# Seven of eight result stores moved from SyncE's queue to GpSimd's in a two-branch attention kernel

## The chip, the cores and the metric

The kernel runs on one core of one Trainium2 chip. The metric is device microseconds from the start to the end of one execution; the comparison value is the median of several runs. Engines are TensorE (PE), VectorE (DVE), ScalarE (ACT), GpSimd (POOL) and SyncE (SP). SP computes nothing here: it issues the transfers between HBM and on-chip memory.

## The reference, cut to what matters

Two attention blocks read their own inputs and their results are put side by side.

```python
def _A_ref(x, k_cache, v_cache, wq, wo):          # 32 query heads, 4 key/value heads
    q = (x @ wq).reshape(B, Sq, Hq, Dh).transpose(0, 2, 1, 3)
    k = jnp.repeat(k_cache, rep, axis=1)          # rep = 8
    v = jnp.repeat(v_cache, rep, axis=1)
    p = _softmax(jnp.einsum("bhqd,bhkd->bhqk", q, k) * (Dh ** -0.5))
    o = jnp.einsum("bhqk,bhkd->bhqd", p, v)
    return o.transpose(0, 2, 1, 3).reshape(B, Sq, Hq * Dh) @ wo
# _B_ref is the same with 32 key/value heads and no repeat
return jnp.concatenate([a, b], axis=-1)
```

B = 16 sequences of Sq = 32 queries, D = 1024, Sk = 1024 keys, Dh = 128, all bf16. Block B's two caches hold 134 MB each and are read once; this is what makes up most of the 337.64 MB that the profile counts as read.

## The kernel before

**Steps.** The work runs in 128 steps (step 0 to 127). Each step handles one B quad (two sequences times two heads) and, a little faster, one A quad (one sequence times four heads), so that A is done with step 123. In the text "scores 124" is the B quad of step 124, "124A" the A quad of that step. For a quad, in this order:

- K arrives in `KB_sb` (8 slots, two transfers of 512 KB a step, line 772; one slot each is called K127a and K127b) and is transposed in place by DVE (line 806);
- PE makes scores into `ps_s` (line 847 for B, 827 for A; two buffers, taken in turn);
- DVE takes the negated maximum (line 857), ACT the exponential into `P_sb` with its sum (line 870);
- PE transposes `P_sb` (line 882), ACT or DVE copies it to `PT_sb` (line 531);
- PE multiplies with V (line 912 for B, 904 for A); V is in `VB_sb` (3 slots of two transfers of 512 KB, line 785);
- the result is scaled into `O_sb` (lines 928, 929), transposed (line 934) and copied to `OTA_sb` or `OTB_sb`.

V of quad n may only be fetched when the V product of quad n-3 has been done, since there are three slots. After four steps of B (eight of A) a group of 128 tokens has all heads of a block of heads, and `oproj` multiplies them with `wo` (line 703: 16 matmuls for A, 8 for B) and adds into the fp32 accumulator `acc`. For the last block of heads the addition (line 717, called accF) writes bf16 back over the front of the accumulator, and the result rows of that group (128 x 1024 bf16, 256 KB) are stored (line 720). There are four groups in A and four in B: eight stores.

**Order.** Every operation is put into a list with its reads and writes. `list_schedule` then simulates all engines with a table of durations and fixes the order on each engine by estimated start, including the order of transfers on SP. Each engine runs its list strictly in order; an operation waits for its semaphores at the head of its engine's list, and everything behind it on that engine waits too. For a store this means: SP stands at the store until DVE has done both accF additions, with the next K and V loads queued behind. All loads and stores are issued by SP and go through one hardware queue (q1). The planner gives a transfer a ready time with a margin:

```python
                if uo.dma_key is not None:
                    r += DMA_MARGIN.get(uo.name, DMA_MARGIN_DEFAULT)
```

At the end SP waits for all transfers. GpSimd makes two identity matrices at the start and then has nothing to do.

Of the kernel before, what the change touches and what calls it, by code (L numbers as in the profile page):

```python
# [10 lines left out]
BF = mybir.dt.bfloat16  # L11
# [429 lines left out]
def build(nc, pa, pb, out):  # L441
    P = 128
    Bn, Sq, D = pa["x"].shape
    NTOK = Bn * Sq
    assert Sq == 32 and Bn % 4 == 0
    NG = NTOK // P
# [21 lines left out]
    out_flat = out.rearrange("b s c -> (b s) c")  # L468
# [3 lines left out]
    cols = [0, D]  # L472

    pr = Prog()
    stack = contextlib.ExitStack()
    with stack:
        def sb(name, shape, dt):
            return stack.enter_context(nc.sbuf_tensor(name, shape, dt))
# [15 lines left out]
        acc = sb("acc", [P, 2, NG, D], F32)  # L494
# [14 lines left out]
        def bank(v):  # L509
            return ps_g[:, v.idx, :]  # L510
# [12 lines left out]
        def evac(dst_ap, src_ap, reads, writes, name, eng=None, wtag=None, rtag=None, mul=None):  # L523
            def emit(e):
                dst = dst_ap() if callable(dst_ap) else dst_ap
                src = src_ap() if callable(src_ap) else src_ap
                if mul is not None:
                    if hasattr(e, "activation"):
                        return e.activation(dst, src, ACTF.Copy, scale=mul)
                    return e.tensor_scalar(dst, src, mul, None, ALU.mult)  # L530
                return e.copy(dst, src) if hasattr(e, "activation") else e.tensor_copy(dst, src)  # L531
            eng = eng or "any"
            pr.add(eng, emit, reads=reads, writes=writes, name=name if eng == "any" else name + "@" + eng, wtag=wtag, rtag=rtag)
# [35 lines left out]
        def lazy_flush(prefix):  # L569
            last = -1  # L570
            for i, (k, _, _) in enumerate(lazy):
                if k[:len(prefix)] == prefix:
                    last = i
            for _ in range(last + 1):
                lazy.pop(0)[1]()
# [113 lines left out]
        def oproj(pi, blk, G):  # L689
            gp = (blk * NG + G) % 2  # L690
            nh = HS if pi == 0 else MS
            nblk = NSB if pi == 0 else NMSB
            OT = OTA_sb if pi == 0 else OTB_sb
            wo_ = woA_sb if pi == 0 else woB_sb
            wo_res = "woA" if pi == 0 else "woB"
            lazy_flush(("wo", pi, blk))
            for oh in range(NOH):
                v = Virt("bank", "pj")
                for h0_ in range(0, nh, 2):
                    def e_op(e, oh=oh, h0_=h0_, v=v):  # L700
                        last = None
                        for hh in range(h0_, h0_ + 2):
                            last = e.matmul(bank(v)[:, 0:OUTW], OT[:, gp, hh, :], wo_[:, hh, oh * OUTW:(oh + 1) * OUTW],  # L703
                                            start=(hh == 0), stop=(hh == nh - 1))
                        return last
                    pr.add("pe", e_op, reads=[("OT", pi, gp, h0_), ("OT", pi, gp, h0_ + 1), (wo_res, h0_), (wo_res, h0_ + 1)], writes=[v],
                           name="oprojA" if pi == 0 else "oprojB",
                           dur=0.45 * OUTW / 512, rtag={(wo_res, h0_): blk, (wo_res, h0_ + 1): blk, ("OTv", pi, gp): (blk, G)})
                a_ap = acc[:, pi, G, oh * OUTW:(oh + 1) * OUTW]
                o_ap = acc[:, pi, G, :].bitcast(BF)[:, oh * OUTW:(oh + 1) * OUTW]  # L710
                if blk == 0:
                    evac(a_ap, lambda v=v: bank(v)[:, 0:OUTW], reads=[], writes=[v, ("acc", pi, G, oh)], name="acc0")
                elif blk < nblk - 1:
                    pr.add("dve", lambda e, a_ap=a_ap, v=v: e.tensor_tensor(a_ap, a_ap, bank(v)[:, 0:OUTW], ALU.add),  # L714
                           reads=[], writes=[v, ("acc", pi, G, oh)], name="acc+")
                else:
                    pr.add("dve", lambda e, a_ap=a_ap, o_ap=o_ap, v=v: e.tensor_tensor(o_ap, a_ap, bank(v)[:, 0:OUTW], ALU.add),
                           reads=[], writes=[v] + [("acc", pi, G, x) for x in range(oh + 1)], name="accF")
            if blk == nblk - 1:
                pr.add("sp", lambda e: e.dma_start(out_flat[G * P:(G + 1) * P, cols[pi]:cols[pi] + D], acc[:, pi, G, :].bitcast(BF)[:, 0:D]),  # L720
                       reads=[("acc", pi, G, x) for x in range(NOH)], dma_key=f"out{pi}_{G}", name="out_dma", dur=P * D * 2)

        class Quad:
# [342 lines left out]
        def stepA(qA):  # L1066
            tA = qA.t % (NG * 8)
            if qA.t == min(1, NIT - 1):
                for hh in pro_heads:
                    qprojA_head(0, hh)  # L1070
                wo_loadA(0)
            quadA_all(qA)
            if qA.last_of_group:
                oproj(0, qA.s, qA.G)
                if qA.G == NG - 1 and qA.s + 1 < NSB:
                    wo_loadA(qA.s + 1)

        for t in range(NIT):
            cur_step[0] = t
            pr.step = t  # L1080
            qB = quadsB[t]
            tB = t % (NG * 4)
            quadB_all(qB)
            target = min(NIT, -(-(t + 1) * NIT // NAS))
            while ia[0] < target:
                stepA(quadsA[ia[0]])
                ia[0] += 1
            tn = t + (4 - t % 4)
            if tn < NIT:
                qn = quadsB[tn]  # L1090
                if t % 4 == 0:
                    qprepB_tr(qn.m, qn.G)
                    qprepB_sh(qn.m, qn.G)
            for what in q_plan.get(t, ()):
                what()
            if qB.last_of_group:
                oproj(1, qB.m, qB.G)
                if qB.G == NG - 1 and qB.m + 1 < NMSB:
                    wo_loadB(qB.m + 1)
            lazy_pop(LAZY_PER_STEP)  # L1100
# [3 lines left out]
        if SCHED:  # L1104
            pr = pr.list_schedule()
# [41 lines left out]
```

## Time and profile before

| what | value |
|---|---|
| median of 3 runs | 891.7 us (891.68 to 892.2) |
| the profiled execution, whole | 894.39 us |
| its span, first to last instruction | 892.3 us |
| PE / DVE / ACT / POOL busy | 92% / 83% / 68% / 0% |
| DMA moved in all | 341.65 MB, mean 383 GB/s over the span |
| mean granted TensorE clock | 0.994 |
| stores: first and last issue | 715.94 us, 888.9 us |
| stores: issue on SP, min / median / max | 0.343 / 0.356 / 1.152 us |

The profiled execution lies 2.7 us above the median, of which the part outside the span is 2.1 us. Times given as "at 871.13" are us from the start of the span. A DMA share at or over 1 means that all 16 DMA engines had work through the whole slice. Single issues on SP last from 0.33 us; much longer ones are read here as standing against a full queue.

### The profile page before, as it was taken

Reading aid. Unit: us, or ns where it says so; the run is one execution under the profiler, and the core shown is the slowest. Engines: PE = TensorE matmul, PEld = TensorE weight load, DVE = VectorE, ACT = ScalarE, POOL = GpSimd, SP = SyncE. Lnnn points to the kernel's source line nnn. Section 1 sums busy time; section 2 is a strip of 40 time slices with the busy share of each in tenths; the row PEclk is TensorE's granted clock in tenths of the full one; section 3 lists DMA queues with packets and bytes.
Section 4 is the critical chain, followed back from the end, with each engine's and each line's share of the span. In section 5 each row is a group of like instructions: output and inputs, shape, how many; then the busy total and the mean of one; then the engine's idle time right before and its main releaser. Section 6 shows DMA issues by size and latency. Waiting matters only on the chain.

```text
span 892.3 us, 29320 instructions
## 1 busy us (share of the span) xinstructions
PE 820.2 (92%) x12864; PEld 469.4 (53%) x12864; DVE 739.5 (83%) x1030; ACT 608.6 (68%) x1347; POOL 1.1 (0%) x8
## 2 busy tenths in 40 slices
PE   6999899999999999999999999999899878978976
PEld 3365565556555455555555555555456545544543
DVE  0398888879987888889898888898899889888985
ACT  3387886776768577675777677676767767565763
POOL 0000000000000000000000000000000000000000
PEclk9999999999999999999999999999999999998999
DMA  9999999999999999999999999999999999999994
GB/s 318 397 395 392 391 393 396 392 389 395 395 366 387 396 395 390 380 393 395 395 393 394 391 393 394 372 395 394 394 378 380 393 395 395 396 394 382 394 374 166
DMA packets 145278, 341.65 MB, mean 383 GB/s; under 512 B 12032, under 2 KB 12032, under 8 KB 145152
## 3 DMA queue, kind: packets, MB, share of 16 engines
q1 hardware_dynamic: 145152, 339.79, 100.7%
q8 instruction: 101, 1.65, 0.8%
q14 instruction: 25, 0.20, 0.1%
HBM read 337.64 MB, written 2.10 MB: 381 GB/s over the span
## 4 chain that ended last, share of the span: by engine, by line
PE 53%; DMA 18%; DVE 14%; ACT 9%; SPq 3%; issue 1%; DVEq 0%; ACTq 0%
DMA KB_sb<-in_B_k_cache_dram 14%; PE ps_s L847 12%; PE ps_g L703 9%; PE ps_g L882 9%; ACT P_sb L870 6%; DVE stat L857 6%; DVE KB_sb L806 6%; PE ps_g L912 5%; PE ps_g L615 4%; PE ps_g L904 4%; PE ps_s L827 3%; PE ps_g L634 3%; PE ps_g L798 2%; ACT PT_sb L531 2%; SPq L785 2%; DMA VB_sb<-in_B_v_cache_dram 1%
## 5 line engine op out<-in xcount | busy, mean ns | idle before, releaser
L857 DVE TENSOR_REDUCE stat<-ps_s 128x1 f32<-128x1024 f32 x256 | 305.4, 1208 | 53.3 <-PE ps_s L847 43.9
L806 DVE STREAM_TRANSPOSE KB_sb<-KB_sb 128x1024 f32<-128x1024 f32 x256 | 310.2, 1230 | 35.8 <-DMA KB_sb<-in_B_k_cache_dram 32.7
L870 ACT ACTIVATE P_sb<-ps_s,stat 128x1024 bf16<-128x1024 f32 x256 | 286.1, 1119 | 60.9 <-DVE stat L857 59.2
L882 PE MATMUL ps_g<-id,P_sb 128*128 128x128 f32 x1024 | 172.7, 295 | 9.7 <-ACT OTA_sb L531 3.2
L847 PE MATMUL ps_s<-KB_sb,QR 32*32 32x512 bf16 x4096 | 160.1, 397 | 23.1 <-ACT P_sb L870 17.4
L882 PEld LDWEIGHTS ps_g<-id,P_sb 128*128 128x128 f32 x1024 | 149.1, 207 | 48.1 <-issue 9.2
L531 ACT COPY PT_sb<-ps_g 128x512 f32<-128x512 f32 x238 | 138.2, 593 | 50.9 <-PE ps_g L882 49.8
L928 ACT ACTIVATE O_sb<-ps_g,stat 128x128 bf16<-128x128 f32 x186 | 67.9, 371 | 62.9 <-PE ps_g L912 36.5
L912 PE MATMUL ps_g<-VB_sb,PT_sb 128*32 128x128 bf16 x4096 | 92.0, 224 | 7.0 <-ACT PT_sb L531 3.6
L847 PEld LDWEIGHTS ps_s<-KB_sb,QR 32*32 32x32 bf16 x4096 | 47.1, 89 | 85.0 <-ACT P_sb L870 27.0
L827 PE MATMUL ps_s<-KTA_sb,QT_sb 128*128 128x512 bf16 x256 | 87.0, 383 | 4.2 <-ACT P_sb L870 4.1
L912 PEld LDWEIGHTS ps_g<-VB_sb,PT_sb 128*32 128x32 bf16 x4096 | 60.5, 97 | 55.3 <-issue 36.4
L904 PE MATMUL ps_g<-VA_sb,PT_sb 128*128 128x128 bf16 x1024 | 77.6, 220 | 3.1 <-ACT PT_sb L531 1.2
L904 PEld LDWEIGHTS ps_g<-VA_sb,PT_sb 128*128 128x128 bf16 x1024 | 61.0, 98 | 31.6 <-issue 13.9
L634 PE MATMUL ps_g<-wq_sb,xT_sb 128*128 128x512 bf16 x256 | 72.8, 388 | 3.9 <-DMA wq_sb<-in_B_wq_dram 3.9
L703 PE MATMUL ps_g<-woB_sb,OTB_sb 128*128 128x512 bf16 x256 | 67.6, 380 | 3.4 <-ACT PT_sb L531 1.3
L703 PE MATMUL ps_g<-woA_sb,OTA_sb 128*128 128x512 bf16 x256 | 62.5, 380 | 0.8 <-DVE OTA_sb L531 0.3
L934 PE MATMUL ps_g<-ident,O_sb 128*128 128x128 bf16 x256 | 52.5, 223 | 4.5 <-ACT O_sb L928 3.6
L615 PE MATMUL ps_g<-xT_sb,wq_sb 128*128 128x512 bf16 x192 | 55.5, 380 | 0.4 <-ACT QR L531 0.2
L870 ACT ACTIVATION_READ_ACCUMULATOR P_sb<-ps_s,stat 128x1 f32 x256 | 51.6, 202 | 0.0
L531 ACT COPY OTA_sb<-ps_g 128x64 f32<-128x64 f32 x114 | 24.5, 216 | 37.2 <-PE ps_g L934 36.6
L714 DVE TENSOR_TENSOR acc<-acc,ps_g 128x512 f32<-128x512 f32 x64 | 41.0, 675 | 8.7 <-PE ps_g L703 8.4
(42 smaller groups left out, 511.9 us busy)
## 6 DMA issues: line engine op xcount, KB each, us to landing
VB_sb<-in_B_v_cache_dram SPq DMA_DIRECT2D x256, 512.0 KB, 12.2
KB_sb<-in_B_k_cache_dram SPq DMA_DIRECT2D x256, 512.0 KB, 12.4
KA_sb<-in_A_k_cache_dram SPq DMA_DIRECT2D x64, 256.0 KB, 12.3
VA_sb<-in_A_v_cache_dram SPq DMA_DIRECT2D x64, 256.0 KB, 12.2
wq_sb<-in_B_wq_dram SPq DMA_DIRECT2D x16, 512.0 KB, 10.5
woB_sb<-in_B_wo_dram SPq DMA_DIRECT2D x32, 256.0 KB, 11.3
woA_sb<-in_A_wo_dram SPq DMA_DIRECT2D x32, 256.0 KB, 9.9
wq_sb<-in_A_wq_dram SPq DMA_DIRECT2D x12, 512.0 KB, 11.3
```

The source lines that it names most:

```text
L531: return e.copy(dst, src) if hasattr(e, "activation") else e.tensor_copy(dst, src)
L615: last = e.matmul(bank(v)[:, 0:tn], w_[:, j, hh * Dh:(hh + 1) * Dh], xT_sb[:, 0, j, t0:t0 + tn], start=(j == 0), stop=(j == DJ - 1))
L634: last = e.matmul(bank(v)[:, 0:CW], xT_sb[:, 1, j, G * P:(G + 1) * P], wq_sb[:, j, mh * CW:(mh + 1) * CW], start=(j == 0), stop=(j == DJ - 1))
L703: last = e.matmul(bank(v)[:, 0:OUTW], OT[:, gp, hh, :], wo_[:, hh, oh * OUTW:(oh + 1) * OUTW], start=(hh == 0), stop=(hh == nh - 1))
L806: pr.add("dve", lambda e: e.transpose(KB_sb[:, sl, :].bitcast(F32), KB_sb[:, sl, :].bitcast(F32)), writes=[("KB", sl)], name="KBt_tr", rta ...
L827: pr.add("pe", lambda e, u=u: e.matmul(ps_s[:, vS.idx, u, :], qt[:, q.b, q.hh0:q.hh0 + 4, :].rearrange("p a q -> p (a q)"), KTA_sb[:, sl, ...
L847: last = e.matmul(ps_s[32 * cg:32 * cg + 32, vS.idx, g2, :].rearrange("p (s j) -> p s j", s=16), lhsT, rhs, start=(fp == 0), stop=(fp == 3 ...
L857: pr.add("dve", lambda e: e.tensor_reduce(stat[:, vst.idx, 0:1], ps_s[:, vS.idx, :, :], AXIS.XY, ALU.max, negate=True), writes=vS.res + [v ...
L870: return e.activation(dst, src, ACTF.Exp, bias=stat[:, vst.idx, 0:1], scale=1.0, accum_out=stat[:, vst.idx, 1:2])
L882: last = e.transpose(bank(vb)[:, m * P:(m + 1) * P], p32[:, m:Sk // 2:NPK], id32[:])
L904: last = e.matmul(bank(vb)[:, 0:Dh], ptc_of(vPT, c, 0, P), VA_sb[:, kvs, c, :], start=(c == 0), stop=(c == NCH - 1))
L912: last = e.matmul(bank(vb)[32 * a:32 * a + 32, 0:Dh], ptc_of(vPT, c, 32 * a, 32 * a + 32), VB_sb[:, kvs, a // 2, a % 2, c, :], start=(c == ...
```

## The change

The store is issued by GpSimd except for the last group of B. Nothing else in the source differs; the order of all engines is planned anew from the new list.

```diff
             if blk == nblk - 1:
-                pr.add("sp", lambda e: e.dma_start(out_flat[G * P:(G + 1) * P, cols[pi]:cols[pi] + D], acc[:, pi, G, :].bitcast(BF)[:, 0:D]),
+                pr.add("sp" if pi == 1 and G == NG - 1 else "pool", lambda e: e.dma_start(out_flat[G * P:(G + 1) * P, cols[pi]:cols[pi] + D], acc[:, pi, G, :].bitcast(BF)[:, 0:D]),
                        reads=[("acc", pi, G, x) for x in range(NOH)], dma_key=f"out{pi}_{G}", name="out_dma", dur=P * D * 2)
```

In the built program GpSimd has seven stores behind its identity matrices, each waiting for DVE, and SP has one. SP's loads stand in the old order up to the tail, where V125 (waiting for the V product of quad 122) comes ahead of the two loads of K127 instead of behind them. On PE, DVE and ACT the order differs in two stretches: around the first two stores (steps 100 to 108) and from about step 121 to the end. In the second, these move:

- PE: the V product of quad 122 stands ahead of that of 123 (it stood behind); the 16 matmuls of A's last `oproj` are mixed with the 8 of B's and stand ahead of scores 125 (they stood behind it, in one piece, ahead of the transposes of quad 124).
- DVE: max 122 stands between the transposes of K123a and K123b (it stood behind both); in the tail the order is accF, accF, K126a, accF, accF, K126b, max 125, K127a, K127b, max 126, max 127 (it was accF, accF, K126a, K127a, K127b, accF, accF, K126b, max 125, max 126, max 127).

## The prediction

> **What bounds the kernel now.** I read the queue's own waits first, since the change takes stores out of SP's list. Columns: us in total, times, longest.
>
> ```profile
> SPq L785 <- PE ps_g L912: 68.3, 33, 6.2
> SPq L785 <- PE ps_s L847: 60.3, 30, 7.8
> SPq L720 <- DVE acc L717: 23.4, 6, 11.0
> ```
>
> SP stands 23.4 us at stores waiting for accF. The 11.0 us is the last store of the kernel, which stays on SP; 12.4 us go. That is worth something only where the DMA engines run dry meanwhile, so the windows come next (PE, PEld, DVE, ACT, POOL busy; clock; DMA share; GB/s).
>
> ```profile
> 712.00:812.00 100.00, 81.54 (x1467) 49.70 (x1455) 89.13 (x124) 66.97 (x149) 0.00 (x0) 0.98 1.04 395
> 812.00:824.00 12.00, 11.97 (x146) 5.61 (x139) 8.92 (x12) 5.22 (x13) 0.00 (x0) 0.91 1.01 369
> 824.00:864.00 40.00, 32.37 (x602) 21.35 (x600) 37.39 (x55) 28.89 (x62) 0.00 (x0) 0.97 1.04 397
> 864.00:888.00 24.00, 20.47 (x360) 10.39 (x359) 15.65 (x22) 10.29 (x25) 0.00 (x0) 0.97 0.61 221
> ```
>
> Up to 864 the DMA engines are full at 395 to 397 GB/s but for one dent, and SP's wait is hidden by transfers already queued. From 864 on they are at 221 GB/s: the tail is no longer set by bandwidth. So I read the tail on SP, PE and DVE in the timeline (start, us).
>
> ```profile
> 855.86 3.71 SPq L772 DMA_DIRECT2D KB_sb<-in_B_k_cache_dram  x4
> 866.99 1.92 SPq L785 DMA_DIRECT2D VB_sb<-in_B_v_cache_dram  x4
> 871.13 0.36 SPq L720 DMA_DIRECT2D out_dram<-acc  x1
> 876.41 0.88 SPq L785 DMA_DIRECT2D VB_sb<-in_B_v_cache_dram  x2
> ```
> ```profile
> 861.90 1.03 PE L912 MATMUL ps_g<-VB_sb,PT_sb 128*32 128x128 bf16 x32 [1.35 <-DMA VB_sb<-in_B_v_cache_dram]
> 870.96 3.63 PE L703 MATMUL ps_g<-woA_sb,OTA_sb 128*128 128x512 bf16 x16
> 874.42 0.63 PE L882 MATMUL ps_g<-id,P_sb 128*128 128x128 f32 x4
> 885.01 0.63 PE L912 MATMUL ps_g<-VB_sb,PT_sb 128*32 128x128 bf16 x32 [0.62 <-ACT PT_sb L531]
> ```
> ```profile
> 871.02 3.49 DVE L806 STREAM_TRANSPOSE KB_sb<-KB_sb 128x1024 f32<-128x1024 f32 x3
> 874.43 1.44 DVE L717 TENSOR_TENSOR acc<-acc,ps_g 128x512 bf16<-128x512 f32 x2
> 875.79 1.24 DVE L806 STREAM_TRANSPOSE KB_sb<-KB_sb 128x1024 f32<-128x1024 f32 x1
> 880.63 1.22 DVE L857 TENSOR_REDUCE stat<-ps_s 128x1 f32<-128x1024 f32 x1 [0.84 <-PE ps_s L847]
> ```
>
> The V product of 123 (861.90) waits for its data, with that of 122, whose data is there, behind it; hence V125 and V126 are issued only at 866.99. A's `oproj` then holds PE in one piece for 3.63 us, its accF comes at 874.43, behind that K126b at 875.79, and then the last three scores. The final max is done at 881.85 and the V product of 127 starts at 885.01, for a copy by ACT and not for a DMA. The end is a chain of engine work in a fixed order, and the change reorders it.
>
> **Part by part. GpSimd's issue.** Seven stores leave SP: issues of 0.36 us (one 1.15 us), some 3.3 us, and 12.4 us of waits. Behind each on SP stood the next K and V loads. At 767 and 843 SP stood 2.7 and 3.6 us, and the DMA stayed full: worth nothing. In 812 to 824 SP stood 2.2 and 1.6 us, and the rate fell to 369 GB/s: (397-369)/397 x 12 = 0.85 us of transfer. Between 824 and 849 the chain of waits runs through engines alone, so I count 0 of it and keep 0.8 for the range. On GpSimd a waiting store holds only the next store. GpSimd's last stores become ready at about 872, 17 us before the end, while a store took at most 11.0 us to land; they end nothing.
>
> **What a GpSimd store costs.** The trace has none. Bounds: below, a gain only if its packets were cheaper than those of SP's store, 0.66 us at 395 GB/s (256 KB), at most 7 x 0.66 = 4.6 us, of which I exclude nearly all, since the bytes and rows are the same. Above, the engines could be held twice as long: 5 stores before the tail, 5 x 0.66 = 3.3 us. The nearest row is SP's own store of the same bytes, so I take 0 and keep part of the 3.3 for the range. The Trainium skill, DMA: Bandwidth & Descriptors, "Issuing engines are not separate DMA queues", says that all issuers share the same 16 engines, and that spreading issues saves only the sequencer's time; by that alone the sum would be 0 (the first rival).
>
> **The new order around the first stores** (716 to about 790). The DMA is full there, and SP's issues of 1 to 4 us show a full queue, so a shift of one or two us on PE costs nothing; 0, at worst a dent like the 0.85 us one.
>
> **The tail**, in the built order and with this trace's durations (transpose 1.16, max 1.2, exp with its sum 1.21, accF 0.69, copy 0.6):
> - DVE from 851.16: K123a, max 122 (to 853.5), K123b, max 122A (855.9). Exp 122 ends at 855.1 where it ended at 856.03; scores 123 to 856.3; max 123 to 857.5; exp 123 to 858.7 where it was 859.74.
> - PE: P 123 transposed by 859.3, then the V product of 122, after its copy, at 859.8 to 860.4. Its slot was free at 866.94. V125 is issued at about 860.5 instead of 866.99, K127 behind it by 863, and the queue doesn't run dry.
> - Max 123, K124a, max 123A, K124b end at 861.0; scores 124 at 862.2 (was 867.3).
> - Then on PE, ahead of P 124: P 123A (0.5), V products 123 and 123A (1.1), two small transposes (0.2), 24 `oproj` matmuls (5.5), scores 125 (1.1): 8.4 us, and 1.0 for waits on the copies into `OTA_sb` and `OTB_sb` (PE's load queue shows 0.9 us for such waits in the tail): scores 125 end at 871.6, `oproj` at 870.5. P 124 is done at 872.2 where it was 875.05, V127 issued at about 874.3 (was 876.41).
> - DVE: last accF pair to 871.9, K126b 873.1, max 125 874.3, K127a and b 876.6, max 126 877.8, max 127 879.0 (was 881.85).
> - Exp 127 to 880.25 (was 883.09). From there to the V product of 127 it was 1.92 us: 882.2 instead of 885.01. V127 landed 4.3 to 5.3 us after issue, so by 880: no wait. Behind it nothing changes: 892.3 - 885.01 = 7.3 us, end of span 889.5.
>
> The gain is 2.8 us: profiled execution 891.6, span 889.5. The median lies 2.7 us under the profiled one: 888.9.
>
> Thinnest cover: K127 now stands behind V125 in the queue. In this stretch K loads took 12.3 to 13.8 us to land, hence K127 by about 871.5 before; 1 MB more ahead at 397 GB/s is 2.6 us: 874.1, needed at 874.3 and 875.4. What it is late goes on the end one for one.
>
> **Rivals.**
> 1. *No change.* The hidden waits are hidden, and the tail's gain of 2.8 us goes into waits that my sum leaves out: in-order ACT (O copies behind exp 124) ahead of the mixed `oproj`, PSUM banks that accF gives back, K127 late by a us. For: each of some fifteen hand-overs needs only 0.1 to 0.15 us more. Against: max 125 alone moves from 876.95 to about 873. Gain 0 to 1.7 us; 891.2.
> 2. *Slower: GpSimd's stores hold the DMA engines.* Place: the 16 engines, full until 864; a second queue takes turns with loads, and loads due next (K125 and V123, for which DVE and PE wait at 862.97 and 861.90) land late by what each store costs beyond its 0.66 us. Five stores come before that point. It decides from (2.8 + 1.8)/5 = 0.9 us extra per store on; at 1.2 us extra, 6.0 - 2.8 = 3.2 us slower, 894.9. Against: no row shows such a cost. The Trainium skill, DMA: Bandwidth & Descriptors, "Latency and other measured facts", calls engines 7 and 15 usually slower and guesses at the ports that hold GpSimd's descriptor rings; that bears on this rival, and no run here shows it yet.
> 3. *More.* The 0.85 us dent comes through as well, and the waits I added are shorter: 3.6 to 4.6 us, 887.6.
>
> That the change doesn't do what it says is excluded by the built order: seven stores stand on GpSimd.
>
> **How the numbers follow.** A measurement of this kernel can tell about 0.2%, 1.8 us, from no change. Forecast 0.47 (888.9, itself 887.5 to 889.9), no change 0.30, slower 0.16, more 0.07. Faster 0.54, same 0.30, slower 0.16. The range goes down to 887.0, past most of "more", and up to 893.5, which takes in "no change" and the mild end of rival 2.
>
> **What would show it.** After: L720 on SP once, with one wait; a dent near 816 smaller than 369 GB/s shows; V125 issued near 860 and V127 near 874; the line-703 matmuls of A ahead of scores 125, in pieces; the last max ending near 879; DMA rate in the tail over 221 GB/s. Wrong if the last max ends at 881 or later, if K127's transposes wait for DMA, or if rate in 824 to 864 falls below 395 GB/s with GpSimd's stores in it (rival 2).

## The result and the profile after

| what | before | after |
|---|---|---|
| median (15 runs each, same chip) | 892.49 us (891.28 to 894.5) | 890.16 us (889.52 to 892.01) |
| ratio of the two, 95% interval | | 0.9974 [0.9966, 0.9982] |
| the profiled execution / its span | 894.39 / 892.3 us | 890.14 / 888.3 us |

The changed kernel is 2.3 us (0.26%) faster; 888.9 us had been predicted. The two profiled spans differ by more, 4.0 us. To know how much of this belongs to the tail, I measure it inside each trace: from the start of the first accF of B's second group, which lies ahead of the stretch that is reordered, to the end of the span. Before it is 892.3 - 841.59 = 50.7 us, after 888.3 - 840.30 = 48.0 us. So 2.7 us come from the tail, where 2.8 had been worked out. The other 1.3 us are lost or won ahead of it and belong to the one execution, not to the change: a run below with the old order reaches the same point at 839.74. All times of after are therefore compared with the predicted ones less 1.3 us. The tail repeats well: 50.6 to 50.8 us in three traces with the old order of the tail (before, and e2 and e8 below), 48.0 to 48.2 in three with the new one (after, e1, e4).

The queue's waits of after (us in total, times, longest) and the groups at line 720 (issue min/median/max, first to last issue; then the time from issue to landing of all stores):

```profile
SPq L785 <- PE ps_g L912: 70.8, 32, 5.7
SPq L785 <- PE ps_s L847: 56.9, 30, 7.8
SPq L720 <- DVE acc L717: 11.2, 1, 11.2
...
L720 POOL DMA_DIRECT2D out_dram<-acc x7: 539/542/682, 712.0 to 870.4; - x7
L720 SPq DMA_DIRECT2D out_dram<-acc x1: 360/360/360, 884.9 to 884.9; - x1
...
DMA to landing us min/median/max: 2.1/6.2/6.7
```

SP stands at one store instead of six, as foreseen: 12.2 us of its waits are gone. The other large waits of SP are for V slots and scores, and the two largest are about as long as before (70.8 and 56.9 us, before 68.3 and 60.3).

The windows of after (PE, PEld, DVE, ACT, POOL busy; clock; DMA share; GB/s):

```profile
712.00:812.00 100.00, 82.68 (x1458) 49.56 (x1460) 88.37 (x124) 66.38 (x148) 1.22 (x2) 0.95 1.04 395
812.00:824.00 12.00, 11.97 (x130) 6.61 (x127) 9.19 (x12) 5.83 (x14) 1.08 (x2) 0.95 1.03 382
824.00:864.00 40.00, 34.05 (x668) 21.87 (x667) 37.01 (x53) 31.17 (x71) 0.54 (x1) 1.00 1.04 395
864.00:888.00 24.00, 15.77 (x281) 7.82 (x279) 13.96 (x20) 7.58 (x19) 1.08 (x2) 1.00 0.55 210
```

Up to 864 the rates are within 2 GB/s of those of before, but for the dent at 812 to 824 (382 instead of 369 GB/s), with five stores of GpSimd among the loads. From 864 to 888 after moves 210 GB/s where before moved 221. The time comes out of the tail, and there the timeline of SP, PE and DVE shows the new order (start, us):

```profile
859.21 0.89 SPq L785 DMA_DIRECT2D VB_sb<-in_B_v_cache_dram  x2
860.15 1.50 SPq L772 DMA_DIRECT2D KB_sb<-in_B_k_cache_dram  x2
864.45 9.19 SPq L785 DMA_DIRECT2D VB_sb<-in_B_v_cache_dram  x4
```
```profile
858.54 0.63 PE L912 MATMUL ps_g<-VB_sb,PT_sb 128*32 128x128 bf16 x32
...
863.10 1.03 PE L703 MATMUL ps_g<-woA_sb,OTA_sb 128*128 128x512 bf16 x4
...
868.64 1.13 PE L847 MATMUL ps_s<-KB_sb,QR 32*32 32x512 bf16 x32
...
880.48 0.63 PE L912 MATMUL ps_g<-VB_sb,PT_sb 128*32 128x128 bf16 x32 [0.33 <-DMA VB_sb<-in_B_v_cache_dram]
```
```profile
868.91 1.25 DVE L717 TENSOR_TENSOR acc<-acc,ps_g 128x512 bf16<-128x512 f32 x2
870.08 1.23 DVE L806 STREAM_TRANSPOSE KB_sb<-KB_sb 128x1024 f32<-128x1024 f32 x1
871.23 1.18 DVE L857 TENSOR_REDUCE stat<-ps_s 128x1 f32<-128x1024 f32 x1
872.54 2.52 DVE L806 STREAM_TRANSPOSE KB_sb<-KB_sb 128x1024 f32<-128x1024 f32 x2
874.99 2.56 DVE L857 TENSOR_REDUCE stat<-ps_s 128x1 f32<-128x1024 f32 x2
```

V125 is issued at 859.21 where it was 866.99. A's `oproj` is done in pieces ahead of scores 125 (868.64); in the eight microseconds that begin 20 us behind the first accF of B's second group, line 703 has PE for 5.56 us where before it had 1.12, and before has 4.41 us of it in the next eight. Max 125 runs at 871.23, ahead of both K127 transposes, and the last max ends at 877.55 instead of 881.85. What the last V product waits for has changed as well: 0.33 us for its data. The new plan also gives some short copies and scalings (lines 531 and 929) to ACT that DVE had: from that first accF to the end DVE does five of them instead of nine.

### The profile page after: what moved, and what is told of

Read it like the earlier page. It is cut to its first block, busy times and chain, and to the rows that moved or that the text cites. A ratio compares the mean times of both kernels' runs of the same rounds, so it can differ in the third digit from the quotient of the medians.

```text
span 888.3 us, 29316 instructions
## 1 busy us (share of the span) xinstructions
PE 819.5 (92%) x12864; PEld 469.1 (53%) x12864; DVE 737.9 (83%) x1027; ACT 608.7 (69%) x1350; POOL 5.1 (1%) x15
## 3 DMA queue, kind: packets, MB, share of 16 engines
q1 hardware_dynamic: 144144, 337.95, 100.5%
q0 software_dynamic: 560, 1.84, 0.5%
## 4 chain that ended last, share of the span: by engine, by line
PE 53%; DMA 19%; DVE 13%; ACT 10%; SPq 3%; issue 1%; ACTq 0%; DVEq 0%
DMA KB_sb<-in_B_k_cache_dram 15%; PE ps_s L847 11%; PE ps_g L703 10%; PE ps_g L882 8%; ACT P_sb L870 6%; DVE stat L857 6%; DVE KB_sb L806 5%; PE ps_g L912 5%; PE ps_g L904 4%; PE ps_g L615 4%; PE ps_s L827 3%; PE ps_g L634 3%; PE ps_g L798 2%; SPq L785 2%; ACT PT_sb L531 2%; DMA KA_sb<-in_A_k_cache_dram 1%
## 5 line engine op out<-in xcount | busy, mean ns | idle before, releaser
L882 PEld LDWEIGHTS ps_g<-id,P_sb 128*128 128x128 f32 x1024 | 148.6, 207 | 49.4 <-issue 8.8
## 6 DMA issues: line engine op xcount, KB each, us to landing
VB_sb<-in_B_v_cache_dram SPq DMA_DIRECT2D x256, 512.0 KB, 12.2
KA_sb<-in_A_k_cache_dram SPq DMA_DIRECT2D x64, 256.0 KB, 12.2
```

Source lines behind the costliest of these rows:

```text
L882: last = e.transpose(bank(vb)[:, m * P:(m + 1) * P], p32[:, m:Sk // 2:NPK], id32[:])
```

## The experiments

The change does two things at once: seven stores stand on another queue, and the planner, given another engine, writes another order (and shares out those copies anew; "order" below means the whole plan). The first two runs take them apart. In these kernels either the order is that of after and all stores are on SP, or the reverse.

**After's order, all stores on SP** (e1; the order is planned as in the changed kernel, then the stores go back to SP):

```diff
-            eng, emit, reads, writes, dma_key, name, dur, tag, prio = self.specs[order[k]]
+            eng, emit, reads, writes, dma_key, name, dur, tag, prio = self.specs[order[k]]; eng = "sp" if name == "out_dma" else eng
```

> All eight stores are issued by SyncE again, but PE, DVE and ACT keep the order that the plan of the changed kernel gave them (on SyncE the stores stand at their planned times). Theory 'order' (the gain is the tail in another order on PE, DVE and SP's loads): 2.0 to 2.8 us faster than before, ratio 0.997 to 0.998, last max some 2 us or more earlier than before's 881.85, the waits of SP at stores back at some 20 us. Theory 'queue' (the gain is that SP no longer stands at stores): no change, ratio 0.9995 to 1.0005. Theory 'both': half, about 0.9985.

Measured: 890.08 us, ratio to before 0.9966 [0.9955, 0.9977], as fast as the change. Its waits on SP and its window at the dent:

```profile
SPq L720 <- DVE acc L717: 25.8, 6, 11.3
```
```profile
812.00:824.00 12.00, 11.97 (x129) 6.45 (x130) 9.30 (x11) 5.55 (x14) 0.00 (x0) 0.94 1.04 395
```

SP stands at stores for 25.8 us again, more than before (11.3 of it at the last store, which is on SP in after too), and no cost can be measured. The tail is 888.6 - 840.59 = 48.0 us, to the tenth that of after. In this run SP stands at stores beside the dent as well, and the rate there is 395 GB/s.

**Before's order, seven stores on GpSimd** (e2; the order planned as before, the stores moved behind it):

```diff
-            eng, emit, reads, writes, dma_key, name, dur, tag, prio = self.specs[order[k]]
+            eng, emit, reads, writes, dma_key, name, dur, tag, prio = self.specs[order[k]]; eng = "pool" if name == "out_dma" and dma_key != "out1_3" else eng
```

> Seven stores are issued by GpSimd, but PE, DVE, ACT and the loads on SP keep the order of before. Theory 'order': 0 to 0.85 us faster (only the dent of 812 to 824, 369 GB/s, can be filled), ratio 0.999 to 1.000, last max still near 881. Theory 'queue': the whole gain, ratio 0.9966 to 0.998. Rival 2 of the prediction (GpSimd's stores hold the DMA engines): slower than before, ratio over 1.001.

Measured: 892.58 us, ratio 0.9999 [0.9989, 1.001]; tail 890.3 - 839.74 = 50.6 us. DVE in its tail:

```profile
868.99 3.49 DVE L806 STREAM_TRANSPOSE KB_sb<-KB_sb 128x1024 f32<-128x1024 f32 x3
872.40 1.44 DVE L717 TENSOR_TENSOR acc<-acc,ps_g 128x512 bf16<-128x512 f32 x2
```

Three transposes stand ahead of A's accF pair, as before. The stores on GpSimd, by themselves, neither gain nor cost anything that can be measured, and the gain is the order, as far as intervals of about 1 us to either side can tell. So the change doesn't work by what its words say.

**One store on GpSimd** (e3, that of B's second group, issued near 842) and **the change once more** (e4):

```diff
-                pr.add("sp", lambda e: e.dma_start(out_flat[G * P:...
+                pr.add("pool" if (pi, G) in ((1, 1),) else "sp", lambda e: e.dma_start(out_flat[G * P:...
```

> Only the store of B's second group goes to GpSimd; the others stay on SP. In the built order the steps 100 to 108 then stand as before and the tail nearly as after. Theory 'order, in the tail': the whole gain but the dent, ratio 0.997 to 0.998. If the gain came from the other order around the first two stores: no change, 1.000. Theory 'queue': one of seven stores, at most a seventh of the gain, 0.9996.

> The changed kernel itself, beside the other three on the same chip: ratio 0.9966 to 0.9982, span some 2.3 to 4 us under before's.

Measured: e3 890.27 us, 0.9969 [0.9958, 0.9981], tail 887.7 - 839.01 = 48.7 us; e4 890.38 us, 0.9971 [0.9961, 0.9982], tail 889.3 - 841.08 = 48.2 us. DVE of e3, max 125 and behind it K127a and K127b:

```profile
871.17 1.19 DVE L857 TENSOR_REDUCE stat<-ps_s 128x1 f32<-128x1024 f32 x1
872.28 2.35 DVE L806 STREAM_TRANSPOSE KB_sb<-KB_sb 128x1024 f32<-128x1024 f32 x2
```

One store is enough: without it in SP's list the planner puts two accF pairs between transposes and max 125 ahead of K127a, as in after, and the gain is there.

The next question is which move in the order carries it. Three kernels keep before's plan, with all stores on SP, and move single operations in the finished list (`put_before` takes operations out of it and puts them ahead of another; the lines below it in the source shift by 10 or 12). A fourth has only the reordering at steps 100 to 108.

**K126b and max 125 ahead of K127a and K127b** (e5):

```diff
+        put_before(where("KBt_tr", 126)[1:] + where("max", 125), where("KBt_tr", 127)[0])
```

> Kernel before with all eight stores on SyncE; one move in the planned order: on DVE, K126b and max 125 stand ahead of K127a, K127b and A's last accF pair. Theory 'DVE queue' (A's accF, which waits for the oproj in one piece, holds up K126b and the last maxima): max 125 from 876.95 to about 873.5, last max 1.1 us earlier, ratio 0.9985 to 0.9990; tail (first accF of B's second group to the end of the span) 50.7 to about 49.6 us. Theory 'PE' (the oproj and the V products on PE set the tail and DVE only follows): no change, 0.9995 to 1.0005, tail 50.7.

Measured: 892.53 us, 0.9997 [0.9985, 1.0008]; tail 892.3 - 842.16 = 50.1 us. DVE and PE in its tail (lines 867, 727, 713, 944 are 857, 717, 703, 934):

```profile
873.50 1.18 DVE L867 TENSOR_REDUCE stat<-ps_s 128x1 f32<-128x1024 f32 x1
876.89 1.44 DVE L727 TENSOR_TENSOR acc<-acc,ps_g 128x512 bf16<-128x512 f32 x2
880.21 1.22 DVE L867 TENSOR_REDUCE stat<-ps_s 128x1 f32<-128x1024 f32 x1 [0.22 <-PE ps_s L857]
```
```profile
871.16 3.63 PE L713 MATMUL ps_g<-woA_sb,OTA_sb 128*128 128x512 bf16 x16
878.85 0.23 PE L944 MATMUL ps_g<-ident,O_sb 128*128 128x128 bf16 x1 [1.23 <-DVE O_sb L939]
```

Max 125 runs at 873.50, but A's `oproj` still has PE in one piece up to 874.8, its accF pair now stands behind the transposes at 876.89, and PE waits 1.23 us for a scaled result behind that on DVE, with the last scores queued behind. Counted from the first accF of B's second group, max 125 is 4.0 us earlier than in before, the last max 1.0 us and the end 0.6 us: most of what was saved on max 125 is lost on the way, and that wait is the longest single one of PE there.

**V product of 122 ahead of that of 123** (e6):

```diff
+        put_before(where("PVB", 122), where("PVB", 123)[0])
```

> Kernel before with all eight stores on SyncE; one move: on PE the V product of quad 122 stands ahead of that of 123 (which waits for V123). V125 is issued near 862 instead of 866.99 by either theory. Theory 'DVE queue': the PE gap of 1.35 us at 861 is partly filled, 0.3 to 0.6 us faster, ratio 0.9993 to 0.9997, tail 50.1 to 50.4. Theory 'V slots' (the late release of the V slots, and so the empty DMA queue at 866, sets the end): most of the gain, ratio 0.997 to 0.998, tail 48.0 to 48.7.

Measured: 892.3 us, 0.9994 [0.9983, 1.0004]; tail 890.2 - 839.95 = 50.3 us. SP and the last max on DVE:

```profile
861.67 3.63 SPq L795 DMA_DIRECT2D VB_sb<-in_B_v_cache_dram  x4
```
```profile
878.47 1.22 DVE L867 TENSOR_REDUCE stat<-ps_s 128x1 f32<-128x1024 f32 x1 [0.83 <-PE ps_s L857]
```

Counted from the first accF of B's second group, V125 and V126 go out 3.7 us earlier than in before, and in the 8 us that begin 20 us behind it, where before moved 333 GB/s, this kernel moves 399. The tail is only 0.4 us shorter. So the less busy queue of before did not by itself set the end.

**Three moves at once** (e7: both of these, and max 122 between K123a and K123b):

```diff
+        put_before(where("KBt_tr", 126)[1:] + where("max", 125), where("KBt_tr", 127)[0])
+        put_before(where("PVB", 122), where("PVB", 123)[0])
+        put_before(where("max", 122)[:1], where("KBt_tr", 123)[1])
```

> Kernel before with all eight stores on SyncE and three moves together: those of the two kernels above, and max 122 ahead of K123b on DVE. If these are what the new plan gained by: 1.7 to 2.7 us faster, ratio 0.997 to 0.998, tail 48.0 to 49.0. If A's oproj mixed with B's ahead of scores 125 (which is not made here) is needed for it: under 1.2 us, ratio over 0.9985, tail over 49.5.

Measured: 891.29 us, 0.9986 [0.9975, 0.9996]; tail 889.2 - 839.39 = 49.8 us. Together they bring 0.9 of the tail's 2.7 us, about what e5 (0.6) and e6 (0.4) bring in their traces one by one. A's `oproj` still stands in one piece (868.00 to 871.63); what of the new tail this kernel lacks is that `oproj` in pieces ahead of scores 125, and what moves with it.

**The first two stores on GpSimd** (e8; new order at steps 100 to 108, old tail):

```diff
-                pr.add("sp", lambda e: e.dma_start(out_flat[G * P:...
+                pr.add("pool" if (pi, G) in ((0, 0), (0, 1)) else "sp", lambda e: e.dma_start(out_flat[G * P:...
```

> Only the first two stores (A's first two groups) go to GpSimd; the built order then has the new stretch around steps 100 to 108 and the old tail. The prediction gave this stretch 0: ratio 0.999 to 1.001, tail 50.7. Rival (the new order there costs or gains something): outside that by more than 0.1%.

Measured: 892.95 us, 1.0001 [0.9991, 1.0012]; tail 890.8 - 840.02 = 50.8 us. The reordering in the stretch where the DMA engines are full is worth nothing that can be measured.

The last question is whether the new tail could be better still. PE has waits in the last 15 us; if A's `oproj` filled them instead of standing ahead of scores 125, the scores would come earlier. The planner is told so with a lower rank for those matmuls, by 6 (e9) or 3 (e10), in the changed kernel:

```diff
-                           dur=0.45 * OUTW / 512, rtag={(wo_res, h0_): blk, ...
+                           prio=-6 if pi == 0 and blk == nblk - 1 and G == NG - 1 else 0, dur=0.45 * OUTW / 512, rtag={(wo_res, h0_): blk, ...
```

> The changed kernel, with one more edit: the planner holds the matmuls of A's last oproj for 6 us less urgent, so that they stand in pieces behind P 124, the V product of 124 and P 125 instead of ahead of scores 125; V127 may be fetched earlier, and DVE has K126a, K126b and max 125 ahead of A's second accF. Theory 'filler' (the tail is set by where the oproj stands on PE): better than the changed kernel by 0.5 to 1.5 us, ratio to before 0.9950 to 0.9968, tail (first accF of B's second group to the end of the span) 46.5 to 47.5 us against 48.0. Theory 'DVE work' (from max 124 on DVE has 14.5 us of work whatever the order): no better than the changed kernel, ratio 0.9966 to 0.9982, tail 47.8 to 48.5.

> As the kernel beside it, with 3 us instead of 6: the oproj of A stands half ahead of scores 125, half ahead of scores 126. Theory 'filler': between the changed kernel and the one with 6 us, ratio 0.9955 to 0.9970, tail 47.0 to 48.0. Theory 'DVE work': 0.9966 to 0.9982, tail 47.8 to 48.5.

Measured: e9 890.4 us, 0.9982 [0.9971, 0.9993]; e10 890.88 us, 0.9978 [0.9969, 0.9986]. Neither is faster than after, and the idea missed. Two lines of e10, DVE and PE:

```profile
872.34 2.52 DVE L806 STREAM_TRANSPOSE KB_sb<-KB_sb 128x1024 f32<-128x1024 f32 x2 [0.73 <-DMA KB_sb<-in_B_k_cache_dram]
876.90 1.23 DVE L857 TENSOR_REDUCE stat<-ps_s 128x1 f32<-128x1024 f32 x1 [0.93 <-PE ps_s L847]
```

The transposes of K127 now wait 0.73 us for their data, and the last max still waits for its scores; the tail is 888.7 - 839.28 = 49.4 us. (The profiled execution of e9, 893.28 us, is the longest of its runs; the clock granted in its last 15 us was 0.79 and 0.72, so its tail of 50.4 us is not compared.)

**All eight stores on GpSimd** (e11):

```diff
-                pr.add("sp", lambda e: e.dma_start(out_flat[G * P:...
+                pr.add("pool", lambda e: e.dma_start(out_flat[G * P:...
```

> The changed kernel with the last store on GpSimd too; nothing else moves. This store ends the kernel, so what a GpSimd store costs more than one of SP is seen in full: 0.18 us more of issue (0.54 against 0.36) and what its descriptors and landing take. Expected 0.2 to 0.8 us slower than the changed kernel, ratio to before 0.9972 to 0.9985, tail 48.2 to 48.8 us. If GpSimd's stores were as quick as SP's: 0.9971, tail 48.0.

Measured: 890.82 us, 0.9979 [0.9969, 0.9988]. Its last accF pair on DVE and the last store:

```profile
885.75 1.48 DVE L717 TENSOR_TENSOR acc<-acc,ps_g 128x512 bf16<-128x512 f32 x2 [4.33 <-PE ps_g L703]
```
```profile
887.52 0.54 POOL L720 DMA_DIRECT2D out_dram<-acc  x1 [14.39 <-DVE acc L717]
```

From the end of that pair to the end of the span it takes 891.3 - 887.23 = 4.1 us, and with the store on SP 888.3 - 884.83 = 3.5 us (after) and 892.3 - 888.83 = 3.5 us (before). Here, where a store does end the program, GpSimd costs 0.6 us in the trace; 0.9979 against 0.9974 doesn't resolve it in the times. None of the versions is faster than the change: e1 and e3 equal it within their intervals.

## Why the prediction was right

The gain came as in the likeliest of its cases, 2.3 us where 2.8 had been worked out, and the cause it gave, the tail's new order, is the one that e1 and e2 isolate. The time itself is less of a hit: 890.16 us lies 0.3 us above that case's own 887.5 to 889.9, and would have fitted its first rival (0 to 1.7 us under 891.7) as well. What tells the two apart is that the median of before rose from 891.7 to 892.49 us with more runs, and that the tail is 2.7 us shorter in the traces. By the forecast's steps, the predicted times less 1.3 us for the execution:

| step | predicted | measured |
|---|---|---|
| V125 issued | 859.2 | 859.21 |
| scores 125 end | 870.3 | 869.77 |
| V127 issued | 873.0 | 873.1 |
| last max ends | 877.7 | 877.55 |
| V product of 127 starts | 880.9 | 880.48 |
| end of span | 888.2 | 888.3 |

- **SP's 12.4 us, counted at nothing.** 12.2 us went, and e1, which has them back, is as fast. Right, within about 1 us.
- **A GpSimd store, taken at 0 between -4.6 and +3.3 us.** e2 has 0.9999 with an interval of about 1 us to either side. The second rival (GpSimd's stores hold the engines) needed 0.9 us extra from each of five stores to turn the sign, 4.5 us; e2 leaves at most about 1 us for all. It fell. The rule of the Trainium skill (DMA: Bandwidth & Descriptors, "Issuing engines are not separate DMA queues"), by which moving issues alone gives nothing here, agrees with e2 (0.9999). No run tested the guess on engines 7 and 15.
- **The first stores' new order, 0.** e8: 1.0001. Right, within about 1 us.
- **The dent at 812 to 824, laid to SP's two waits (0.85 us, kept for the range).** Not borne out. e1 has the waits and 395 GB/s; after, without them, has 382. Over all traces the rate of these 12 us differs from execution to execution, from 369 to 397 GB/s. In before, the clock granted to PE was low just there (0.58 in 804 to 808, 0.84 and 0.73 in the next two slices), but in e1 it was low too (0.76 and 0.82 in 808 to 816) and the dent is missing; no run tested the clock as its cause, and the cause stays open. The third rival, built on the dent, has no support.
- **No wait of the last V product for its data.** Wrong. V127 was expected 4.3 to 5.3 us after issue and took 7.2. The chain of work that ended last in after shows it:

```profile
873.10 0.01 SPq L785
873.15 7.19 DMA VB_sb<-in_B_v_cache_dram
880.48 0.66 PE ps_g L912 x32
```

  It cost 0.33 us, since the V product would have been ready at 880.15, sooner than the 880.9 worked out. So the chain that ends the changed kernel runs through V127's slot and its transfer, and not through the last max as in the forecast's sum. Why V127 took longer to land than in before is not shown.
- **Nothing changes behind the last V product, 7.3 us.** It took 888.3 - 880.48 = 7.8 us, since PE now waits for a copy by ACT ahead of the last `oproj`:

```profile
881.74 0.61 PE L703 MATMUL ps_g<-woB_sb,OTB_sb 128*128 128x512 bf16 x2 [0.47 <-ACT OTB_sb L531]
```

  That the end of the span comes out to 0.1 us is in part luck: the V product starts 0.4 us earlier than worked out, and what follows it is 0.5 us longer.
- **The thinnest cover, K127.** It held to a few tenths of a microsecond. In after, K127a starts 1.31 us after max 125 starts, in e3, where nothing waits, 1.11 us. In e1, with the order of after, the view names the wait:

```profile
872.83 2.53 DVE L806 STREAM_TRANSPOSE KB_sb<-KB_sb 128x1024 f32<-128x1024 f32 x2 [0.32 <-DMA KB_sb<-in_B_k_cache_dram]
```

  In e11 it is 0.40 us and in e10 0.73 us. So the sign "K127's transposes wait for DMA" did appear, too small to take the gain away.
- **DMA rate in the tail over 221 GB/s.** It didn't come: 210 in 864 to 888. The sign was a poor one. At 864 the execution of after is 1.3 us further on than that of before, which at 395 GB/s is 0.5 MB less left to move, more than the difference of the two rates over 24 us (0.26 MB).
- **The first rival (the gain is lost in waits that the sum leaves out).** In after scores 125 ended 0.5 us earlier than summed, so the hand-overs up to there took no more than the 1.0 us that the sum allowed. But something like it happened to e5 and e6, where a part of the order was made alone: each puts operations earlier by about 4 us, and 0.6 and 0.4 us of that reach the end.

What stays open: the three moves of e7 give 0.9 us of the 2.7; the other 1.8 us come from the rest of the new plan, and no run shows from which part. A's `oproj` ahead of scores 125 is its largest piece, and e9 and e10 show that later is no better, but it wasn't made alone, since its results share PSUM banks with other work of the list.

The size was near as well: 2.3 us measured against 2.8 (interval of the measured gain 1.6 to 3.0). The median of before rested on three runs; more runs of the same kernel have medians of 892.4 to 893.1 us and reach from 890.8 to 895.1, so a forecast of the time itself carries about a microsecond from that alone. A small part of the gain lies outside the span, which the forecast left as it was: whole execution less span is 1.79 us on average in the runs of e4 and 2.04 us in those of before beside them. No run shows why.

## What to carry to other kernels

Where a planner fixes the order of all engines, a change of one operation's engine is also a change of the plan: compare the two built orders before costing the operation, and test order and placement apart, by moving the operation after the plan is made. Waits of the issuing engine (25.8 us in e1) need not cost anything while transfers issued earlier still keep the DMA engines busy; look at the DMA rate beside them first. In a tail that is a chain across engines, an early link that is moved alone may gain little (in e5 4.0 us on one max, 0.6 us at the end), so work out the whole chain up to the last instruction, the last transfer included.

## What the runs showed of the hardware

- The issue of a store of 256 KB took 0.54 us on GpSimd and 0.36 us on SP (medians). Beside full loads a store issued by GpSimd landed sooner: of the five stores between 711 and 850, those on GpSimd landed 5.5 to 6.7 us after issue (after, e11), those on SP 7.2 to 11.0 us (before, e1). That a store on SP's queue stands behind the loads issued ahead of it would fit this; no run tests it.
- The same seven stores are 560 packets in the profile's list of queues on GpSimd's queue, and took 1008 out of the list of SP's (145152 to 144144), for the same 1.84 MB. No run shows a difference in time from that.

```profile
q1 hardware_dynamic: 144144, 337.95, 100.5%
...
q0 software_dynamic: 560, 1.84, 0.5%
```
